# Turning three more expert steps' x by transposing DMAs in a fused linear-attention and mixture-of-experts kernel

## The chip, the cores and the metric

The kernel runs on one core of a Trainium2 chip. The metric is the device time of one execution in microseconds (us). The median of 3 runs before the change is 637.44 us (637.18 to 638.03).

## What is computed

The reference is a linear attention with random features, followed by a top-1 mixture of experts over all 4608 tokens. Everything is float32.

```python
def phi(x):                                    # q and k, scaled; omega: 128 x 64
    h = einsum('bhsd,md->bhsm', x, omega) - sum(x * x) / 2
    return exp(h - max(h)) / sqrt(m)
kv, z = einsum('bhsm,bhsd->bhmd', k_p, v), sum(k_p, axis=2)
attn = (q_p @ kv) / (q_p @ z + 1e-06)          # 8 x 8 x 576 x 64
x = attn.transpose(0, 2, 1, 3).reshape(4608, 512)

logits = normalised(x) @ normalised(expert_emb).T / tau    # 8 experts
expert_idx = argmax(logits, axis=1)
gate_w = softmax(logits)[arange(N), expert_idx]
for e in range(8):
    mask = expert_idx == e
    h = maximum(x[mask] @ w1[e], 0.0)                      # 512 -> 1024
    out[mask] = gate_w[mask, None] * (h @ w2[e])           # 1024 -> 512
```

## The kernel before

The first part computes the attention and scatters each token's row of x to a buffer in HBM (`xs`), sorted by expert. The second part, which the change touches, is a row of expert steps. A step takes 128 token rows of one expert. Steps 0 and 1 run inside the first part; the loop at L1177 runs steps t = 2 to 37 (`NPRE` = 2, `NSTAT` = 38).

Every float32 product is made of three: each operand is split into a high part and a low part (`xh`, `xl`; `hh`, `hl`; `w1h`, `w1l`, `w2h`, `w2l`), and `products` (L274) issues high by high, high by low-weight, and low by high-weight, for each of four slices of 128 rows. Half of a step's hidden layer is thus 12 matmuls of 512 columns, `pa[0]` and then `pa[1]` (`pb` in the trace), and the product with w2 is 24 (`po`). The first two matmuls of a half need only `xh`, the third needs `xl`.

TensorE contracts over partitions, so x must be turned (128 rows x 512 columns into four 128 x 128 blocks, transposed) and so must h. There are two ways to do it:

- On TensorE: `x_turned` (L1032) calls `turned` (L263): four transposes into a PSUM bank, ScalarE writes `xh` (L267), VectorE writes `xl` (L268).
- By DMA: `apart16` (L1078) copies the upper and lower 16 bits of every float32 into two planes `pl_1` and `pl_0`; `turned16` (L1086) issues one transposing DMA for each plane on SyncE's queue (L1090), into `t_k_0` and `t_k_1` of step k; in the next step `rejoin` (L1098) puts the two halves together in `wd`, and `summed` (L1113) makes `xh` (L1116), `hh` (L1118), `xl` (L1121) and `hl` (L1122).

Step t's own h goes by DMA in all steps but the first and the last. Where `far` holds, x of step t + 2 rides along in the same two planes, as 4 more blocks beside the 8 of h; elsewhere x of the next step is turned on TensorE between the two halves of a step. These are the lines:

```python
far = XPE <= t + 2 < NSTAT                                                 # L1179
planes = None if near else [... f"pl{t}_{k}", tag=f"pl{k}", bufs=1 ...]    # L1219
if t == NPRE or NPRE + 1 < t < XPE - 1:
    xt[t + 1] = x_turned(t + 1, xg[t + 1])                                 # L1223
if far:
    apart16(xg[t + 2][:, 0:DM], planes, F)                                 # L1232
if t == SHIFT:
    inverted(totals[0])
    ended()
elif t != SHIFT:
    down(u, both)                                                          # L1270
xg[t + 3] = x_of(t + 3, reg("row", t + 3))                                 # L1278
```

The order on every engine is the order in which the code is written. The product with w2 runs one step behind the one with w1 (`u = t - 1`) until step 4 and two steps behind from step 6 on. Step 5 (`SHIFT` = 5) has none: its 24 matmuls with w1 are followed directly by those of step 6. In its place step 5 scales the results of steps 2 and 3 on VectorE (`ended`, L291) ahead of `summed`. x of step t + 3 is loaded (`xgp` or `xg` from `xs`, L186) at the end of step t, behind that step's two transposing DMAs on the same queue.

Of the kernel before, what the change touches and what calls it, by code (L numbers as in the profile page):

```python
# [52 lines left out]
FILL1, FILL2, FILL3 = 2, 4, 8  # L53
NSTAT = 38
NSTEP = 64
XPE = 9
SHIFT = 5
BIGID = 1048576.0
EPS = 1e-6 * M
# [5 lines left out]
def attention_moe(ctx: ExitStack, tc: tile.TileContext, qT, kT, v1, omT, emb, tau, w1q, w2q, xs, out):  # L65
# [148 lines left out]
    def computed(wn, t, ms):  # L214
        for m in ms:
            seq[m] = len(seq)
        for o in range(NSTAT):
            apart(wn, spl.get((wn, o), ()), o, ms, t)
        if t >= NQ and (wn, t) not in mmi:
            for w in spl[wn, t - 1]:  # L220
                tc.add_manual_dep(ms[0].ins, w.ins.name, sync, reason="the weights")
        mmi.setdefault((wn, t), []).extend(ms)
# [51 lines left out]
    def products(dst, a, wn, par, cs, half, begin, end):  # L274
        ah, al = a
        _, wh, wl = W[wn]
        done = []
        for i, c in enumerate(cs):
            for k, (x, w) in enumerate(((ah, wh), (ah, wl), (al, wh))):
                if wn == "w1":  # L280
                    ws = w[:, ds(par, 1), c, half * 512 : (half + 1) * 512]
                else:
                    ws = w[:, ds(par, 1), c // 2, (c % 2) * 512 : (c % 2 + 1) * 512]
                done.append(nc.tensor.matmul(  # L284
                    dst, x[:, c * P : (c + 1) * P], ws.rearrange("p o f -> p (o f)"),
                    start=(begin and i == 0 and k == 0), stop=(end and i == len(cs) - 1 and k == 2),
                ))
        return done
# [743 lines left out]
    def x_turned(t, xg):  # L1032
        xh, xl = sums(t, "x", DM)
        turned(xg, 0, bank(f"pt{t}", "px", 2), xh, xl)
        return xh, xl
# [58 lines left out]
    with tc.manual_schedule(engines={ET.PE, ET.Activation, ET.DVE, ET.Pool, ET.SP}):  # L1094
# [82 lines left out]
        for t in range(NPRE, NSTAT):  # L1177
            u = t - 1 if t < SHIFT else t - 2
            far = XPE <= t + 2 < NSTAT  # L1179
            near = t in (NPRE, ends)  # L1180
# [41 lines left out]
            computed("w1", t, products(pa[0], xt[t], "w1", par, low, 0, True, True))  # L1222
            if t == NPRE or NPRE + 1 < t < XPE - 1:  # L1223
                xt[t + 1] = x_turned(t + 1, xg[t + 1])
# [139 lines left out]
```

## Time and profile before

| | |
|---|---|
| median of 3 runs | 637.44 us |
| profiled execution, its own time | 641.91 us |
| its span, first to last instruction | 640.3 us |
| TensorE (PE) busy | 627.2 us, 98% of the span |
| VectorE (DVE) busy | 491.8 us, 77% |
| ScalarE (ACT) busy | 431.8 us, 67% |
| GpSimd (POOL) busy | 420.6 us, 66% |
| mean granted TensorE clock | 0.998 of full |

The profiled execution is one execution, 4.5 us above the median of the others; its span is 1.6 us shorter than its own time. Times in views count from the start of the span. An engine's busy time does not count its waits; where a row ends with [a time <- a name], the engine was idle for that long ahead of it, and the name is what released it. Matmuls overlap in the pipeline, so the start of one to the start of the next is their cost, not the length shown.

### The profile page before, as it was taken

The page shows a single profiled execution, that of the slowest core. Times are in us where ns is not written, and L with a number is a line of the kernel's source. Part 1 is how long each engine was busy: PE and PEld are TensorE (multiplying, and loading weights), DVE is VectorE, ACT ScalarE, POOL GpSimd, SP SyncE. Part 2 cuts the span into 40 slices and gives each one's busy share as a digit, 9 for nine tenths or more (in the row PEclk, how much of TensorE's full clock was granted, in tenths as well). Part 3 has the DMA queues.
Part 4 walks back from the last instruction along what each step waited for, and adds up shares of the span by engine and source line. Part 5 has one row for each costly group of instructions (what it writes and reads, how often), then busy time and mean ns, then how long its engine had stood idle before and what let it go on. Part 6 is the DMA issues. An engine that isn't in the chain of part 4 may idle for free.

```text
span 640.3 us, 19056 instructions
## 1 busy us (share of the span) xinstructions
PE 627.2 (98%) x6289; PEld 535.4 (84%) x6290; DVE 491.8 (77%) x908; ACT 431.8 (67%) x1139; POOL 420.6 (66%) x603
## 2 busy tenths in 40 slices
PE   9999999999999899999999999999999999999996
PEld 8899999988888688888888888888888888888885
DVE  5688888898879755687778887787778786878754
ACT  6898898898988426755666675757565756666630
POOL 3012443355777644569789797979797979798852
PEclk9999999999999999999999999999999999999999
DMA  7655664767772277978877788686869686878631
GB/s 255 199 153 163 216 209 154 233 203 229 271 270 100 101 239 275 264 183 242 210 237 200 210 232 245 185 256 172 245 184 236 208 237 200 229 218 216 201 116 46
DMA packets 142239, 131.93 MB, mean 206 GB/s; under 512 B 106742, under 2 KB 106870, under 8 KB 142144
## 3 DMA queue, kind: packets, MB, share of 16 engines
q1 hardware_dynamic: 135520, 109.70, 59.7%
q0 software_dynamic: 6480, 20.91, 8.4%
q8 instruction: 57, 0.93, 0.6%
q14 instruction: 38, 0.31, 0.2%
q10 hardware_dynamic: 144, 0.07, 0.0%
HBM read 83.78 MB, written 21.97 MB: 165 GB/s over the span
## 4 chain that ended last, share of the span: by engine, by line
PE 70%; ACT 2%; DVE 1%; DMA 1%; issue 0%; POOL 0%; ACTq 0%
PE pb L284 31%; PE po L284 31%; PE fs_o L284 2%; PE pb L373 1%; PE nuu L481 1%; ACT ftq L387 1%; PE pb L266 1%; PE fs_a L284 1%; DMA rf<-w2q 1%; PE kva L405 1%; PE pb L461 0%; DVE nmq L377 0%; DVE xr L500 0%; PE nuu L538 0%; PE nuu L461 0%
## 5 line engine op out<-in xcount | busy, mean ns | idle before, releaser
L239 POOL TENSOR_TENSOR w2l<-raww,w2h 128x256 f32 x128 | 143.3, 1120 | 7.6
L239 POOL TENSOR_TENSOR w1l<-raww,w1h 128x256 f32 (+1 forms) x130 | 112.5, 865 | 14.5 <-DMA xgp<-xs 5.2
L284 PE MATMUL po<-w2h,hh 128*128 (+1 forms) x288 | 112.2, 390 | 0.0
L284 PE MATMUL po<-w2h,hl 128*128 (+1 forms) x288 | 112.1, 389 | 0.0
L284 PE MATMUL po<-w2l,hh 128*128 (+1 forms) x288 | 112.1, 389 | 0.0
L284 PE MATMUL pb<-w1h,xh 128*128 (+1 forms) x280 | 109.4, 391 | 0.0
L284 PE MATMUL pb<-w1h,xl 128*128 (+1 forms) x280 | 109.0, 389 | 0.0
L284 PE MATMUL pb<-w1l,xh 128*128 (+1 forms) x280 | 109.0, 389 | 0.0
L1084 DVE COPY pl<-pb 128x512 uint16<-128x512 uint16 x68 | 46.7, 689 | 60.2 <-ACT pl L1080 55.9
L1080 ACT ACTIVATE pl<-pb 128x512 uint16<-128x512 uint16 x68 | 39.4, 585 | 76.3 <-PE pb L284 66.5
L314 POOL DMA_INDIRECT y<-xgp,tail x36 | 45.0, 1250 | 55.2 <-DVE w1h L233 28.8
L387 ACT ACTIVATE ftq<-pb,nmq 128x128 f32<-128x128 f32 x288 | 79.6, 429 | 2.2 <-DVE nmq L377 1.3
L387 ACT ACTIVATE ftk<-pb,nmk 128x128 f32<-128x128 f32 x272 | 76.6, 479 | 6.0 <-DVE nmk L377 4.3
L1102 DVE COPY wd<-t 128x1024 uint16<-128x1024 uint16 x68 | 65.4, 963 | 1.6 <-DMA t<-pl 1.5
L1118 ACT ACTIVATE hh<-wd 128x1024 fp32r<-128x1024 f32 x34 | 36.1, 1063 | 42.7 <-DVE wd L1102 38.1
L284 PEld LDWEIGHTS po<-w2h,hh 128*128 128x128 f32 x288 | 54.1, 188 | 11.2
L284 PEld LDWEIGHTS po<-w2l,hh 128*128 128x128 f32 x288 | 54.1, 188 | 11.2
L284 PEld LDWEIGHTS po<-w2h,hl 128*128 128x128 f32 x288 | 54.0, 187 | 11.2
L284 PEld LDWEIGHTS pb<-w1h,xl 128*128 128x128 f32 x280 | 52.6, 188 | 11.0
L284 PEld LDWEIGHTS pb<-w1l,xh 128*128 128x128 f32 x280 | 52.6, 188 | 10.9
L284 PEld LDWEIGHTS pb<-w1h,xh 128*128 128x128 f32 x280 | 52.5, 187 | 10.7
L1122 DVE SCALAR_TENSOR_TENSOR hl<-wd,hh 128x1024 fp32r<-128x1024 f32 x34 | 54.2, 1594 | 4.0 <-ACT hh L1118 3.4
(341 smaller groups left out, 1250.4 us busy)
## 6 DMA issues: line engine op xcount, KB each, us to landing
raww<-w1q SPq DMA_DIRECT2D x38, 512.0 KB
raww<-w2q SPq DMA_DIRECT2D x38, 512.0 KB
qt<-qT SPq DMA_DIRECT2D x36, 256.0 KB
kt<-kT SPq DMA_DIRECT2D x35, 256.0 KB
xg<-xs SPq DMA_DIRECT2D x23, 260.5 KB
xgp<-xs SPq DMA_DIRECT2D x15, 260.5 KB
rf<-w1q SPq DMA_DIRECT2D x4, 512.0 KB
rf<-w2q SPq DMA_DIRECT2D x4, 512.0 KB
```

The lines of the kernel that those rows point to most:

```text
L239: ils.append(eng.tensor_tensor(at(l, d)[:, c], raw[:, c], at(h, d)[:, c].bitcast(F32), op=ALU.subtract))
L266: nc.tensor.transpose(bank[:, c * P : (c + 1) * P], src[:, o + c * P : o + (c + 1) * P], ident)
L284: done.append(nc.tensor.matmul(dst, x[:, c * P : (c + 1) * P], ws.rearrange("p o f -> p (o f)"), start=(begin and i == 0 and k == 0), stop ...
L314: w = nc.gpsimd.indirect_dma_start(out=out, out_offset=bass.IndirectOffsetOnAxis(ap=(xg[:, DM:] if tail is None else tail)[:, E : E + 1].b ...
L373: nc.tensor.matmul(st["pj" + w, i, a][:, c, :], st[w, i][r, c, :], om[r, :], start=True, stop=True)
L387: nc.scalar.activation(ft[:, h, :], pj[:, h, :], AF.Exp, bias=nm[:, h : h + 1])
L405: nc.tensor.matmul(acc[c : c + 64, h, :], ft[:, h, c : c + 64], vt[:, 2 * h + a, :], start=begin and h == 0, stop=u == 4 + 4 * b and h == 3,)
L1080: nc.scalar.activation(planes[1][:, o : o + 512], halved(src)[:, :, 1], AF.Copy)
L1084: nc.vector.tensor_copy(planes[0][:, o : o + 512], halved(src)[:, :, 0])
L1102: nc.vector.tensor_copy(to, src)
L1118: nc.scalar.activation(hh, wd[:, 0:F], AF.Relu)
L1122: nc.vector.scalar_tensor_tensor(hl, wd[:, 0:F], 0.0, hh.bitcast(F32), op0=ALU.max, op1=ALU.subtract)
```

## The change

The constant that says from which step on x is turned by DMA goes from 9 to 6.

```diff
@@ -53,7 +53,7 @@
 FILL1, FILL2, FILL3 = 2, 4, 8
 NSTAT = 38
 NSTEP = 64
-XPE = 9
+XPE = 6
 SHIFT = 5
 BIGID = 1048576.0
 EPS = 1e-6 * M
```

So x of steps 6, 7 and 8 (x6, x7, x8) are no longer turned on TensorE in steps 5, 6 and 7, but ride in the planes of steps 4, 5 and 6. The transposing DMAs of those steps carry 12 blocks where they carried 8. The three `turned` calls go: 12 transposes on TensorE, three L267 on ScalarE, three L268 on VectorE. For each of the three, ScalarE gets two plane copies of x (L1080, L1082), two rejoining copies (L1104) and `xh` (L1116), and VectorE gets `xl` (L1121).

VectorE's queue in step 5 before, from the weight copy that opens the step to the last instruction for step 4's h (`pb` the PSUM banks, `po` the results of steps 2 and 3):

```order
L233 COPY w1h<-raww_5_5426 128x1024
L268 TENSOR_TENSOR xl_5655<-pb_74,xh_5654 128x512
L1084 COPY pl_0_5640<-pb_72 128x512
L1102 COPY wd_5676<-t_4_0_5581 128x1024
L1084 COPY pl_0_5640<-pb_73 128x512
L1102 COPY wd_5676<-t_4_1_5583 128x1024
L307 TENSOR_SCALAR totalb_5628<-totalb_5628 128x3
L308 RECIPROCAL totalb_5628<-totalb_5628 128x3
L291 TENSOR_SCALAR xgp_135<-po_5378,totalb_5628 128x512
L291 TENSOR_SCALAR xgp_136<-po_5587,totalb_5628 128x512
L1122 SCALAR_TENSOR_TENSOR hl_5696<-wd_5676,hh_5695 128x1024
```

The same queue at the same place after the change:

```order
L233 COPY w1h<-raww_5_5426 128x1024
L1084 COPY pl_0_5642<-pb_72 128x512
L1102 COPY wd_5672<-t_4_0_5583 128x1024
L1084 COPY pl_0_5642<-pb_73 128x512
L1102 COPY wd_5672<-t_4_1_5585 128x1024
L307 TENSOR_SCALAR totalb_5630<-totalb_5630 128x3
L308 RECIPROCAL totalb_5630<-totalb_5630 128x3
L291 TENSOR_SCALAR xgp_135<-po_5378,totalb_5630 128x512
L291 TENSOR_SCALAR xgp_136<-po_5589,totalb_5630 128x512
L1121 TENSOR_TENSOR xl_5694<-wd_5672,xh_5693 128x512
L1122 SCALAR_TENSOR_TENSOR hl_5697<-wd_5672,hh_5696 128x1024
```

The low part of x6 was the second of these rows and is now the tenth, behind the plane copy of the step's second half (the second L1084).

ScalarE's queue in step 5 after the change, from the last gate of the step to `hh` (`xg_5193` holds x7, `t_4` the turned planes of step 4; before, one L267 and the two L1080 from `pb` stood ahead of L1118):

```order
L304 ACTIVATE ex_5635,totalb_5630<-tail_5423,nrmb_5624 128x8
L1080 ACTIVATE pl_1_5643<-pb_72 128x512
L1080 ACTIVATE pl_1_5643<-xg_5193 128x512
L1082 ACTIVATE pl_0_5642<-xg_5193 128x512
L1104 ACTIVATE wd_5672<-t_4_0_5583 128x512
L1104 ACTIVATE wd_5672<-t_4_1_5585 128x512
L1080 ACTIVATE pl_1_5643<-pb_73 128x512
L1116 ACTIVATE xh_5693<-wd_5672 128x512
L1118 ACTIVATE hh_5696<-wd_5672 128x1024
```

Five rows are new here, and the copies of x7 now stand ahead of the second half's plane copy.

## Rows read from the trace of the kernel before

**Rows 1.** The page's first part: busy us, share, instructions of each engine.
```profile
PE 627.2 (98%) x6289; PEld 535.4 (84%) x6290; DVE 491.8 (77%) x908; ACT 431.8 (67%) x1139; POOL 420.6 (66%) x603
```

**Rows 2.** Waits of TensorE, longest first: total us, times, longest.
```profile
PE nuu L481 <- DVE base L551: 1.6, 1, 1.6
```

**Rows 3.** Chain that ended last, steps 4 to 8: start us, us, what.
```profile
262.87 5.44 PE po L284 x24
268.31 2.73 PE pb L284 x12
271.04 0.44 PE pb L266 x4
271.48 5.51 PE pb L284 x24
...
285.63 2.72 PE pb L284 x12
...
297.00 5.44 PE pb L284 x24
```

**Rows 4.** SyncE's queue in time order: x6's load, step 4's transposing DMAs.
```profile
258.96 0.33 SPq L186 DMA_DIRECT2D xgp<-xs  x1
...
265.10 2.61 SPq L1090 DMA_TRANSPOSE t<-pl  x2
```

**Rows 5.** ScalarE in time order, steps 4 and 5: start us, us, operation.
```profile
262.98 1.07 ACT L1080 ACTIVATE pl<-pb 128x512 uint16<-128x512 uint16 x2
...
266.07 0.60 ACT L295 ACTIVATE nuu<-xgp 128x512 f32<-128x512 f32 x1
...
268.99 0.19 ACT L304 ACTIVATION_READ_ACCUMULATOR ex<-tail,nrmb 128x1 f32 x1
```

**Rows 6.** L186 (loads of x), 240 to 300 us: issue to landing.
```profile
DMA to landing us min/median/max: 3.1/5.1/7.0
```

**Rows 7.** ScalarE in step 8, where x already goes by DMA.
```profile
300.30 0.62 ACT L1080 ACTIVATE pl<-xg 128x512 uint16<-128x512 uint16 x1
...
301.35 1.41 ACT L1104 ACTIVATE wd<-t 128x512 uint16<-128x512 uint16 x2
...
303.08 0.63 ACT L1116 ACTIVATE xh<-wd 128x512 fp32r<-128x512 f32 x1
```

**Rows 8.** VectorE in step 8, from the second half's plane copy.
```profile
303.21 0.69 DVE L1084 COPY pl<-pb 128x512 uint16<-128x512 uint16 x1 [1.41 <-ACT pl L1080]
...
304.46 1.21 DVE L1121 TENSOR_TENSOR xl<-wd,xh 128x512 fp32r<-128x512 f32 x1
```

**Rows 9.** VectorE in step 5: what follows its last rejoining copy.
```profile
276.16 0.16 DVE L307 TENSOR_SCALAR totalb<-totalb 128x3 f32<-128x3 f32 x1
...
276.56 1.41 DVE L291 TENSOR_SCALAR xgp<-po,totalb 128x512 f32<-128x512 f32 x2
```

**Rows 10.** SyncE's queue in a later step: transposing DMAs, next load.
```profile
467.13 3.00 SPq L1090 DMA_TRANSPOSE t<-pl  x2
470.70 0.34 SPq L186 DMA_DIRECT2D xg<-xs  x1
```

**Rows 11.** ScalarE behind the DMAs of rows 10, in time order.
```profile
473.84 0.60 ACT L1080 ACTIVATE pl<-pb 128x512 uint16<-128x512 uint16 x1 [2.60 <-DMA t<-pl]
474.81 0.63 ACT L1080 ACTIVATE pl<-xg 128x512 uint16<-128x512 uint16 x1 [0.37 <-DMA xg<-xs]
```

**Rows 12.** Stretches: us, busy of PE, PEld, DVE, ACT, POOL; clock, DMA share, GB/s.
```profile
635.00:637.80 2.80, 0.18 (x1) 0.00 (x0) 0.00 (x0) 0.69 (x1) 1.14 (x2) 1.00 0.02 7
637.90:640.00 2.10, 0.00 (x0) 0.00 (x0) 0.00 (x0) 0.00 (x0) 0.00 (x0) 0.50 0.30 106
```

**Rows 13.** TensorE's first matmuls, L91 and L373: ns min/median/max, first to last start.
```profile
L91 PE MATMUL pb<-one x24: 289/314/314, 1.3 to 3.7; 128*128 128x128 bf16 x24
...
L373 PE MATMUL pb<-om,kt x18: 417/418/578, 4.1 to 6.2; 64*128 64x128 f32 x18
...
L373 PE MATMUL pb<-om,kt x34: 272/272/462, 6.2 to 11.9; 64*128 64x128 f32 x34
```

## Prediction

> **What bounds the kernel now.** I read the busy times first: TensorE is busy for 98% of the span, no other engine for more than 77% [rows 1]. Then its waits: the longest single one is 1.6 us, in the attention part [rows 2], so in the expert steps it hardly waits at all. Then the chain that ended last, from step 4 to step 8 [rows 3]: it is TensorE without a gap, one row's end being the next one's start. Step 4's product with w2 runs from 262.87, step 5's first half from 268.31, x6's four transposes at 271.04, then 24 matmuls that are step 5's second half and, with nothing between, step 6's first. So each us taken from TensorE here is a us gained, and each us it waits is lost, since no later row shows idle time that could give it back.
>
> **What is removed.** Step 7, with transposes, goes from 285.63 to 297.00: 11.37 us. A step without them is twice the 5.44 us of 24 matmuls [rows 3], 10.88 us. That is 0.49 us a step (0.44 of transposes and a little of a slower restart), 1.47 us for three. ScalarE's L267 and VectorE's L268 that went with them were off the path.
>
> **What is added, and where it is late.** In a step from 8 on, x of two steps ahead has a step and a half to be turned. The place to look at is step 5, which has no product with w2: x6's new path must fit between step 4's planes and step 6's first half, and the latter is due right behind step 5's second half. Without transposes step 5's 24 matmuls go from 268.31 to 273.75 [rows 3], so step 6's third matmul, the first that needs the low part of x6, is due at 273.75 + 0.45 (two matmuls of 0.227) = 274.2. I follow x6 to that point.
>
> 1. *x6 must be in.* Its load is issued at 258.96 [rows 4]. Loads of x in this stretch take 3.1 to 7.0 us [rows 6], so it lands no earlier than 262.1; ScalarE reads it at 266.07 without a wait [rows 5], which is the upper bound. The new plane copies stand behind the first of two L1080 that start at 262.98, so they want x6 at 263.5. I take a landing at 265.0, near the upper end, because two weight loads stand just ahead of it in the queue.
> 2. *Step 4's planes.* Two copies of x take 1.05 us (300.30 to 301.35 in step 8 [rows 7]): 265.0 to 266.05; the second half's own copy about 0.55 [rows 5]: 266.6. VectorE's copy of the same half waits for ScalarE's each time [rows 8], and takes 0.69: the planes are full at 267.3, and SyncE issues the transposes at 267.4 instead of 265.10 [rows 4]. ScalarE's remaining work of the step, which ended at 269.18 [rows 5], moves by about 2.3 too, to 271.5, where the first half of step 5 is ready (268.31 + 2.73 + 0.4).
> 3. *x7's load* is queued behind the transposes on SyncE. In a later step it is issued 3.57 us after them [rows 10], so at 271.0 here. There ScalarE was held by it until 474.81, 4.1 us after its issue [rows 11]; the least in this stretch is 3.1 [rows 6]. I take 3.1, since only a short queue is left at this point: 274.1. The planes themselves are free once the transposes have read them, at most 6.7 us after their issue (467.13 to 473.84 [rows 10, 11]) and thus no later than x7.
> 4. *ScalarE in step 5.* x7's copies 274.1 to 275.1, the two rejoining copies for x6 1.3 (301.35 to the next start, of 1.41 [rows 7]): 276.4, the second half's plane copy 0.55: 276.9.
> 5. *VectorE in step 5.* Its plane copy and rejoining copy take 1.25 up to the start of the next (303.21 to 304.46 [rows 8]); then come the totals and the two scalings of finished results, 276.16 to 277.97 = 1.81 [rows 9]; then x6's low part, 1.21 [rows 8]. Sum 4.27: 281.2.
>
> So step 6's third matmul starts at 281.2 instead of 274.2: TensorE waits 7.0 us, in two pieces around two early matmuls (xh6 is there at about 277.5, from the 0.63 us of rows 7). Of this, at least 4.8 us need no DMA to be late: step 5's second half ends at 273.75 + 0.4, and 0.55 + 4.27 us of copies behind it in the two queues end at 279.0. The net is 7.0 - 1.47 = +5.5 us. With x6 in by 263.5 and x7 3.1 us after its issue the same sum ends at 279.7 (+4.0); with x6 at 266.07 and x7 4.1 us after its issue it ends at 283.2 (+7.5).
>
> **What is late next.** h of step 4 follows x6 by one VectorE instruction and is used only after step 6's 24 matmuls, 5.4 us later: covered. x7's low part, by the same chain (x8's load issued at about 281.2, 4.1 us to land, then 1.05 + 1.3 + 0.55 + 1.25 + 1.21), is there at 290.7; step 6 has its product with w2 again, so step 7's third matmul is due at 281.2 + 2.3 + 2.7 + 5.4 + 0.45 = 292.1. That cover is 1.4 us; were it gone, each us would be paid. x8 in step 7 is as the steps from 8 on. GpSimd's splitting of the weights waits for the two scalings and moves with them by about 2 us, TensorE by more. The growth of the transposing DMAs from 8 to 12 blocks is in the times of step 3 of the sum, which are those of 12 blocks [rows 10, 11].
>
> **The clock.** At the end of the run TensorE's last matmul reaches 0.18 us into the stretch from 635.00, and from 637.90 on the granted clock reads 0.50, the lower level of 1.2 GHz; over the stretches before it, it is 1.00, and the wait of 1.6 us [rows 2] did not lower it [rows 12]. The wait that I forecast is of 7 us with two matmuls in it, far nearer to the end of the run than to the 1.6 us. What a fall costs: at the start TensorE works from 1.3 us, its L373 take 418 ns until 6.2 and 272 after [rows 13]. Those 4.9 us at half speed bound the loss at 2.5 us; below it is nothing. I take 1.8, nearer to the start's case.
>
> The Trainium skill, TensorE: Matmul & The Clock Gate, section What's actually happening, says that the throttled state is the default and activity lifts it. The end of this trace agrees (0.50 after the last matmul). By that rule the sum is 5.5 + 1.8 = 7.3 us; by the shorter wait's row alone it would stay at 5.5.
>
> **The sum.** On the profiled execution's own 641.91 us: 641.91 + 7.3 = 649.2. On the median, which is 4.5 us lower and holds the same instructions: 637.44 + 7.3 = 644.7 us. Within 0.2% (1.3 us) of 637.44 a measurement of this kernel could hardly tell a change from none.
>
> **The rivals.**
> - *The wait comes, the clock holds.* Two matmuls in the middle of the wait speak for it, the end of the run against it. 642.9 us.
> - *All is hidden.* x6's low part is in time, and TensorE gains its transposes: 637.44 - 1.47 = 636.0. For it: from step 8 on the same path causes no wait, and VectorE and ScalarE have idle time. Against it: it decides at a wait of 1.47 us, that is at xl6 written by 275.7, and VectorE's queue puts it behind a copy that cannot start before step 5's second half has ended at 274.1; it would take 1.6 us for what the rows cost at 4.8.
> - *Only the part that needs no late DMA.* x6 and x7 land early in the changed traffic: wait 4.8 us, net +3.3, so 640.8 with the clock held and 642.6 with a fall.
> - *It spreads.* x7 is late for step 7 too, because x8's load lands 7.0 us after its issue rather than 4.1: 2.9 us later against 1.4 of cover, 1.5 us more, 646.2.
>
> **How the numbers follow.** The wait with a fall of the clock: 0.55, its own range 642.5 to 646.5. The wait, clock held: 0.2. Only the unavoidable part: 0.12. Spread: 0.06. Hidden: 0.04, and 0.03 for something that ends within 0.2%. Range 640.8 to 646.6: it leaves out the hidden and unchanged cases and half of the spread one. Slower 0.93, same 0.03, faster 0.04.
>
> **What would show it.** In the changed trace, TensorE idle ahead of step 6 for 5 to 9 us in all, ended by VectorE's L1121; ScalarE's L1080 on x6 and x7 each with a wait for the load; transposes of step 4 issued near 267.4; steps 6 to 8 at 10.88 us each where the clock is 1.00; a stretch at 0.50 behind the wait. If the gap is under 2 us, the reading of step 5's queues is wrong. If the clock stays at 1.00, only its term is.

## The result and the profile after

The changed kernel takes 645.09 us, median of 5 runs (643.46 to 646.48), and the one before, run beside it, 637.3 (637.14 to 638.03): a ratio of 1.0114, 95% interval 1.0101 to 1.0128. By the medians the change costs 7.8 us, by the ratio 7.3. The forecast was 644.7 in 640.8 to 646.6.

The profiled execution took 643.46 us, with a span of 641.9, only 1.6 more than that of before. In the page's busy line TensorE has 3.3 us less than in [rows 1] and ScalarE 8.4 more.

```profile
PE 623.9 (97%) x6277; PEld 532.9 (83%) x6278; DVE 493.2 (77%) x908; ACT 440.2 (69%) x1151; POOL 420.1 (65%) x603
```

The spans can't be set against each other as they stand. These are the first matmuls of step 4's product with w2 and of step 5, before:

```profile
262.71 0.39 PE L284 MATMUL po<-w2h,hh 128*128 128x512 f32 x1
...
268.15 0.39 PE L284 MATMUL pb<-w1h,xh 128*128 x1
```

And after:

```profile
258.21 0.39 PE L284 MATMUL po<-w2h,hh 128*128 128x512 f32 x1
...
263.65 0.39 PE L284 MATMUL pb<-w1h,xh 128*128 x1
```

All that comes ahead of step 4's product, which the change does not touch, went 4.5 us faster in this execution. (The chain of [rows 3] puts each start 0.16 us later than the matmul's own row.) From that product to the end of the span it is 641.9 - 258.21 = 383.7 us after and 640.3 - 262.71 = 377.6 before. The change costs 6.1 us in this execution.

TensorE's waits, longest first (total us, times, longest): both of the first two are new, the wait of 1.6 us in [rows 2] is of 0.4 us in this execution.

```profile
PE pb L284 <- issue: 3.0, 1, 3.0
PE pb L284 <- DVE xl L1121: 1.9, 1, 1.9
```

TensorE in order of time around them. The first row is step 5's last matmul, the second and third are step 6's first two, the fourth is the third matmul, which needs the low part of x6; the row behind it shows the pitch then, and the last is the first of step 6's product with w2.

```profile
268.87 0.39 PE L284 MATMUL pb<-w1h,xl 128*128 x1
272.21 0.77 PE L284 MATMUL pb<-w1h,xh 128*128 x1 [2.96 <-issue]
272.78 0.63 PE L284 MATMUL pb<-w1l,xh 128*128 x1
275.32 0.79 PE L284 MATMUL pb<-w1h,xl 128*128 x1 [1.92 <-DVE xl L1121]
...
276.34 0.63 PE L284 MATMUL pb<-w1l,xh 128*128 x1
276.77 0.63 PE L284 MATMUL pb<-w1h,xl 128*128 x1
...
282.07 0.39 PE L284 MATMUL po<-w2h,hh 128*128 x1
```

Step 5 begins at 263.65. The third matmul of step 6 was due 5.44 (24 matmuls) + 0.45 = 5.89 us later, at 269.54. It starts at 275.32: a wait of 5.8 us. From there to the product with w2 are 22 matmuls, 4.99 us at 0.227, and they take 6.75: another 1.76 us, since for a part of them the pitch is 0.43. Less the 1.47 us of transposes the sum is 5.8 + 1.76 - 1.47 = 6.1 us, all that the span from step 4's product on shows.

SyncE, ScalarE and VectorE in the same stretch, in order of time. SyncE issues step 4's transposing DMAs, then x7's load:

```profile
262.74 2.88 SPq L1090 DMA_TRANSPOSE t<-pl  x2
265.86 0.38 SPq L186 DMA_DIRECT2D xg<-xs  x1
```

ScalarE takes x6 in the first row as its load lands, then waits for the transposing DMAs to leave the planes, then for x7's load; x6's rejoining, the second half's plane copy and `xh` follow.

```profile
260.35 0.63 ACT L1080 ACTIVATE pl<-xgp 128x512 uint16<-128x512 uint16 x1 [0.99 <-DMA xgp<-xs]
...
267.71 0.60 ACT L1080 ACTIVATE pl<-pb 128x512 uint16<-128x512 uint16 x1 [0.87 <-DMA t<-pl]
268.73 0.63 ACT L1080 ACTIVATE pl<-xg 128x512 uint16<-128x512 uint16 x1 [0.42 <-DMA xg<-xs]
269.27 0.61 ACT L1082 ACTIVATE pl<-xg 128x512 uint16<-128x512 uint16 x1
269.79 1.38 ACT L1104 ACTIVATE wd<-t 128x512 uint16<-128x512 uint16 x2
271.03 0.57 ACT L1080 ACTIVATE pl<-pb 128x512 uint16<-128x512 uint16 x1
271.50 0.62 ACT L1116 ACTIVATE xh<-wd 128x512 fp32r<-128x512 f32 x1
```

VectorE waits for that plane copy, and x6's low part stands behind the two scalings:

```profile
271.63 0.69 DVE L1084 COPY pl<-pb 128x512 uint16<-128x512 uint16 x1 [1.94 <-ACT pl L1080]
272.24 0.74 DVE L1102 COPY wd<-t 128x1024 uint16<-128x1024 uint16 x1
...
273.26 1.41 DVE L291 TENSOR_SCALAR xgp<-po,totalb 128x512 f32<-128x512 f32 x2
274.59 0.68 DVE L1121 TENSOR_TENSOR xl<-wd,xh 128x512 fp32r<-128x512 f32 x1
```

Read backwards, this is the chain that the prediction followed: `xl` behind the scalings, behind the copies, behind ScalarE, behind x7's load. TensorE's first wait, for which the view names only "issue", is ScalarE's `xh`: it ends at 272.12, and the matmul starts at 272.21.

The granted clock, in stretches (us, busy of PE, PEld, DVE, ACT, POOL; clock, DMA share, GB/s):

```profile
262.00:269.20 7.20, 7.20 (x33) 5.66 (x31) 5.19 (x9) 5.72 (x16) 5.04 (x6) 1.00 0.81 207
269.20:272.00 2.80, 0.05 (x1) 0.00 (x0) 0.86 (x2) 2.80 (x6) 1.04 (x1) 1.00 0.10 38
272.00:275.30 3.30, 1.19 (x2) 0.50 (x2) 3.23 (x8) 2.39 (x6) 0.99 (x1) 0.50 0.59 133
275.30:278.80 3.50, 3.48 (x8) 2.80 (x9) 2.48 (x3) 1.09 (x2) 3.13 (x3) 0.50 1.05 265
278.80:282.20 3.40, 3.40 (x16) 2.77 (x16) 1.37 (x2) 2.67 (x5) 3.17 (x5) 1.00 0.99 358
```

At 272.0 it falls to 0.50, the lower level of 1.2 GHz, and it is back at 2.4 GHz from 278.8. In the last row but one 8 matmuls fill 3.48 us; in the last 16 fill 3.40.

From step 6's product with w2 on, the steps have no wait any more, and step 7 takes 10.88 us (5.44 + 5.44), as a step without transposes has to (start us, us, what):

```profile
282.23 5.44 PE po L284 x24
287.67 5.44 PE pb L284 x24
293.11 5.44 PE po L284 x24
```

### The profile page after: what moved, and what is told of

It is laid out like the page before. It is cut to its first block, busy times and chain, and to the rows that moved or that the text cites. A ratio compares the mean times of both kernels' runs of the same rounds, so it can differ in the third digit from the quotient of the medians.

```text
span 641.9 us, 19044 instructions
## 1 busy us (share of the span) xinstructions
PE 623.9 (97%) x6277; PEld 532.9 (83%) x6278; DVE 493.2 (77%) x908; ACT 440.2 (69%) x1151; POOL 420.1 (65%) x603
## 4 chain that ended last, share of the span: by engine, by line
PE 63%; ACT 4%; DVE 2%; DMA 2%; issue 2%; POOL 1%; SPq 0%; DVEq 0%; ACTq 0%; POOLq 0%
PE po L284 29%; PE pb L284 28%; PE fs_o L284 2%; PE pb L373 1%; ACT ftq L387 1%; PE nuu L481 1%; DMA xgp<-xs 1%; DMA raww<-w2q 1%; PE fs_a L284 1%; PE kva L405 1%; DMA xg<-xs 0%; DVE nmq L377 0%; POOL w2l L231 0%; POOL y L314 0%; ACT pl L1080 0%
## 5 line engine op out<-in xcount | busy, mean ns | idle before, releaser
L239 POOL TENSOR_TENSOR w2l<-raww,w2h 128x256 f32 x128 | 143.1, 1118 | 7.6
L239 POOL TENSOR_TENSOR w1l<-raww,w1h 128x256 f32 (+1 forms) x130 | 111.8, 860 | 14.5 <-DMA xgp<-xs 4.8
L1084 DVE COPY pl<-pb 128x512 uint16<-128x512 uint16 x68 | 46.9, 691 | 68.7 <-ACT pl L1080 68.7
L1080 ACT ACTIVATE pl<-pb 128x512 uint16<-128x512 uint16 x68 | 39.6, 584 | 76.6 <-PE pb L284 75.6
L1102 DVE COPY wd<-t 128x1024 uint16<-128x1024 uint16 x68 | 68.4, 1009 | 1.2 <-DMA t<-pl 1.2
L1118 ACT ACTIVATE hh<-wd 128x1024 fp32r<-128x1024 f32 x34 | 36.1, 1062 | 40.8 <-DVE wd L1102 36.6
## 6 DMA issues: line engine op xcount, KB each, us to landing
xg<-xs SPq DMA_DIRECT2D x23, 260.5 KB, 2.9
xgp<-xs SPq DMA_DIRECT2D x15, 260.5 KB, 3.4
```

What stands on the lines that cost most here:

```text
L239: ils.append(eng.tensor_tensor(at(l, d)[:, c], raw[:, c], at(h, d)[:, c].bitcast(F32), op=ALU.subtract))
L1080: nc.scalar.activation(planes[1][:, o : o + 512], halved(src)[:, :, 1], AF.Copy)
L1084: nc.vector.tensor_copy(planes[0][:, o : o + 512], halved(src)[:, :, 0])
L1102: nc.vector.tensor_copy(to, src)
L1118: nc.scalar.activation(hh, wd[:, 0:F], AF.Relu)
```

## The experiments

The first theory: x6 is late because step 5 has no product with w2; only x6 is, so with x7 and x8 by DMA alone the kernel gains two steps' transposes. The rivals: every x costs a third of the loss; x7 is late as well, hidden behind x6's wait; or the clock and not the wait is most of the loss. All edits below are to the changed kernel, unless another is named; a line of dots stands for lines left out. The ratios are to the kernel before, run beside each, and are not the quotients of the two medians (e7's is 0.1% below its quotient): its medians were 637.54 us for e1 to e4, 637.96 for e5 to e8, 638.12 for e9 to e11 and 638.23 for e12.

| run | us, median (range) | ratio, 95% interval |
|---|---|---|
| e1, DMA from x7 on | 642.3 (639.15 to 644.02) | 1.0076, 1.0061 to 1.0091 |
| e2, from x8 on | 638.29 (637.08 to 639.77) | 1.0007, 0.9998 to 1.0017 |
| e3, x6 but not x7, x8 | 645.41 (644.12 to 646.51) | 1.0113, 1.0098 to 1.0129 |
| e4, filling matmuls, shared tile | 650.22 (649.37 to 651.31) | 1.0196, 1.0181 to 1.0212 |
| e5, filling matmuls, free bank | 642.43 (641.96 to 642.84) | 1.0072, 1.0059 to 1.0085 |
| e6, scalings behind `summed` | 643.45 (641.89 to 643.67) | 1.0076, 1.0064 to 1.0089 |
| e7, x6 rejoined first | 643.49 (640.0 to 646.06) | 1.0077, 1.0051 to 1.0103 |
| e8, x6 and x7 first | 639.97 (638.45 to 642.45) | 1.0029, 1.0017 to 1.004 |
| e9, all x first, from x6 | 639.25 (637.78 to 643.15) | 1.0018, 1.0004 to 1.0032 |
| e10, all x first, from x7 | 638.83 (636.82 to 640.8) | 1.0011, 0.9998 to 1.0024 |
| e11, all x first, from x9 | 637.9 (637.0 to 639.29) | 0.9993, 0.9984 to 1.0003 |
| e12, as e9, w1 split earlier | 638.34 (637.05 to 644.48) | 1.0004, 0.998 to 1.0028 |

**Which x is late: e1, e2, e3.**

```diff
-XPE = 6
+XPE = 7
```

> The constant is 7: x6 is turned on TensorE again, x7 and x8 go by DMA. Theory (the wait is x6's alone, because step 5 has no product with w2 to cover its path): no wait, two times 0.49 us of transposes gained, 636.3 us beside 637.3 before. Rival (every x that goes by DMA in these early steps costs a third of the 7.8 us lost, through busier queues): 642.5.

The theory failed: x7 and x8 by DMA cost 4.8 us (642.3 - 637.5), and it is x7, since x8 alone costs nothing that can be told (e2). In e1's trace TensorE waits before step 7, twice. The first row is step 6's last matmul:

```profile
279.95 0.39 PE L284 MATMUL po<-w2h,hl 128*128 x1
282.12 0.47 PE L284 MATMUL pb<-w1h,xh 128*128 x1 [1.77 <-POOL w2l L239]
...
283.50 0.50 PE L284 MATMUL pb<-w1h,xl 128*128 x1 [0.68 <-DVE xl L1121]
```

ScalarE shows the same order as before step 6, one step later, with 1.73 us of waiting for x8's load:

```profile
278.62 0.63 ACT L1080 ACTIVATE pl<-xg 128x512 uint16<-128x512 uint16 x1 [1.73 <-DMA xg<-xs]
...
281.40 0.62 ACT L1116 ACTIVATE xh<-wd 128x512 fp32r<-128x512 f32 x1
```

The first wait is put down to GpSimd, but its row (279.05, 3.16 us) runs to 282.21, past the matmul's start; `xh` of x7 ends at 282.02, 0.10 us ahead of it, and is what it waited for. Step 7's third matmul was due three matmuls behind the first row, at 280.63, and comes at 283.50: 2.9 us late. (The idle times in the rows are shorter, since they count from the end of a matmul's own length.) Less 0.98 of transposes that is 1.9 us. In the profiled execution the clock held, and from step 4's product with w2 on it is 2.1 us longer than before (637.6 - 257.92 = 379.7); that execution is the run of 639.15. The other runs show a mean clock of 0.996 to 0.997. A fall of the clock would explain a part of the median's further 2.7 us: e7's trace, below, has a mean clock of 0.997 and loses 1.7 us by one. No trace of e1's other runs was taken, so the rest is open.

```diff
-XPE = 6
+XPE = 8
```

> The constant is 8: only x8 goes by DMA. Theory: one time 0.49 us gained, 636.8 us, which is only just to be told from 637.3. Rival (a third of the loss for each x): 639.9.

With x8 alone there is no wait in the steps, and the rest of the span is 635.7 - 258.57 = 377.1 us, 0.5 less than before, one step's transposes. The medians don't show it: 1.0007, and the interval reaches from a small gain to a loss of 0.17%.

```diff
-XPE = 6
+XPE = 9
...
-            far = XPE <= t + 2 < NSTAT
+            far = XPE <= t + 2 < NSTAT or t + 2 == 6
...
-            if t == NPRE or NPRE + 1 < t < XPE - 1:
+            if t == NPRE or NPRE + 1 < t < XPE - 1 and t + 1 != 6:
```

> Only x6 goes by DMA, x7 and x8 are turned on TensorE. Theory: nearly the whole loss stays. ScalarE is no longer held by x7's load in step 5, so the wait is some 1.2 us shorter than the 5.8 of the changed kernel, the clock falls as there for some 1.8, and 0.49 is gained: 4.6 + 1.8 - 0.5, 643.2 us. Rival (a third for each x): 639.9.

x6 alone costs as much as all three (645.41 against 645.09), in place of 643.2 expected. The wait is what it was expected to be without x7's load in ScalarE's queue: the third matmul is 4.5 us late, in the two pieces below, where the first again is `xh` (272.69 for 0.62 us), not GpSimd.

```profile
273.41 0.47 PE L284 MATMUL pb<-w1h,xh 128*128 x1 [1.68 <-POOL w1l L239]
...
276.53 0.80 PE L284 MATMUL pb<-w1h,xl 128*128 x1 [2.41 <-DVE xl L1121]
```

So x7's load and its two plane copies in ScalarE's queue are worth 5.8 - 4.5 = 1.3 us of x6's wait. The rest came from the clock: it fell to 0.50 in the second wait and stayed there through step 6's first half; less the 0.49 us of transposes, what the 4.5 us leave of this execution's +6.6 is some 2.5 us for it. (From step 4's product with w2 on it is 644.9 - 260.70 = 384.2 us long, 6.6 more than before.) Together: x7 (with x8) costs 4.8, x6 alone 7.9 (645.41 - 637.5), all three 7.8 (645.09 - 637.3). That is not a third for each x, though e1 came near that rival's 642.5. The waits don't add, since x6's wait gives x7 the time that it lacks (e7 shows it).

**Is the clock's part separate: e4, e5.** 96 matmuls of 128 columns fill TensorE's wait. They leave the results alone. This is e5's edit:

```diff
+            if t == SHIFT + 1:
+                for _ in range(96):
+                    nc.tensor.matmul(pa[1][:, 0:P], one16, one16, start=True, stop=True)
```

In e4 they stood at the end of step 5 and wrote into `nu[1]`.

> The changed kernel with 96 matmuls of 128 columns into an unused PSUM bank between step 5 and step 6, about 5 us of work in a wait of 5.8; they leave the results alone. Theory (the wait and the lower clock behind it are two costs): the clock stays at 1.00, the wait stays, and the time is lower by about 1.8 us than the changed kernel's 645.1, so 643.3. Rival (the clock costs nothing that the wait does not cost already): 645.1. A third possibility is that the matmuls themselves end after the low part of x6 is there; then the time is higher by what they overrun.

It missed its aim: `nu[1]` is the tile into which ScalarE's squares (L295) write, so the added matmuls waited 5.84 us for these and then ran for 8.29 us on the path. It tells nothing of the clock. e5 writes into a bank that is free there.

> The changed kernel with the 96 added matmuls of 128 columns written into the bank of step 6's second half, which nothing reads at that time, ahead of step 6's first matmul. At the 56 ns from start to start that they took at the clock of 1.00 they are 5.4 us in a wait of 5.8. Theory: no clock below 1.00 behind step 5, the low part of x6 comes when it came, the time is lower by the 1.8 us of the clock than 645.1: 643.3. Rival (the clock costs nothing that the wait does not cost): 645.1.

In e5's trace the mean clock is 1.00, so it did not fall in the steps:

```profile
core 0: 640.4 us, clock 1.000
```

TensorE around the filler:

```profile
269.11 5.53 PE L1224 MATMUL pb<-one 128*128 128x128 bf16 x96
...
275.44 0.50 PE L284 MATMUL pb<-w1h,xl 128*128 x1 [0.28 <-DVE xl L1121]
```

The third matmul starts as late as without the filler: 11.8 us behind step 5's first (263.66), against 11.7. The median falls by 645.09 - 642.43 = 2.7 us (the ratio by 0.0042, the same 2.7). From step 4's product with w2 on, the profiled execution is 640.4 - 258.22 = 382.2 us long, 1.5 less than the changed kernel's. So the clock is a term by itself: 1.5 to 1.8 us by the rows of the profiled executions, 2.7 by the medians.

**Is it the order in the queues: e6, e7, e8.** e6 puts the scalings behind `xl`:

```diff
-            if t == SHIFT:
-                inverted(totals[0])
-                ended()
 ...
+            if t == SHIFT:
+                inverted(totals[0])
+                ended()
```

> The changed kernel with the two scalings of step 5 and their totals behind step 4's h on VectorE instead of ahead of x6's low part. Theory (VectorE's queue is part of the wait): the low part comes 1.7 us sooner, 645.1 - 1.7 = 643.4. Rival (the DMAs alone decide when it comes): 645.1.

The median falls by 1.6 us, as expected, and the third matmul comes 10.1 us behind step 5's first (264.06), in place of 11.7: the two scalings stood in x6's way.

```profile
274.18 0.79 PE L284 MATMUL pb<-w1h,xl 128*128 x1 [0.68 <-DVE xl L1121]
```

But a fall of the clock has no fixed price. From the third matmul to the product with w2, at 282.18, e6's 22 matmuls take 8.0 us in place of 4.99: the lower clock costs 3.0 us in this execution, where it cost 1.76 in the changed kernel's. So from step 4's product on e6's is 642.0 - 258.62 = 383.4 us long, only 0.3 less. It is the slowest of e6's six runs.

e7 moves x6's rejoining, `xh` and `xl` ahead of the first plane copy of step 5, and so ahead of x7's load too:

```diff
+                if t in (5,):
+                    wd6 = words(t - 1)
+                    for k in range(2):
+                        rejoin(t - 1, wd6, F, F + DM, k)
+                    xt[t + 1] = xh, xl = sums(t + 1, "x", DM)
+                    nc.scalar.activation(xh, wd6[:, F:], AF.Copy)
+                    nc.vector.tensor_tensor(xl, wd6[:, F:], xh.bitcast(F32), op=ALU.subtract)
                 apart16(pa[0], planes, 0)
...
```

> The changed kernel with x6's rejoining copies, its high and its low part ahead of all plane copies in step 5. Step 4's transposing DMAs landed 2 us before step 6's first half was due, so the DMAs do not forbid it. Theory (the order of the two queues, not the DMAs, makes x6 late): x6's wait falls from 5.8 to about 0.7 us. x7's wait in front of step 7, which the one in front of step 6 hid, comes out then, some 3 us as in the kernel with the constant 7, some of its runs with a fall of the clock: 637.5 - 1.5 + 0.7 + 3.3 = 640.0, with a fall 641.5. Rival (the DMAs make x6 late): 645.1.

x6 is in time, and x7's wait comes out, as e1 foretold, with the clock at 0.50 for a stretch behind it. TensorE's rows are before step 6 (one wait) and before step 7 (two):

```profile
273.00 0.50 PE L284 MATMUL pb<-w1h,xh 128*128 x1 [0.87 <-POOL w1l L239]
...
285.43 0.47 PE L284 MATMUL pb<-w1h,xh 128*128 x1 [1.25 <-POOL w2l L239]
...
286.99 0.79 PE L284 MATMUL pb<-w1h,xl 128*128 x1 [0.86 <-DVE xl L1121]
```

The wait before step 6 is not x6's any more. Its low part (L1235, from 271.67, 0.69 us) is written at 272.36, where it was due at 266.53 + 5.89 = 272.42; GpSimd's low part of the next w1 ends at 272.94:

```profile
269.32 3.62 POOL L239 TENSOR_TENSOR w1l<-raww,w1h 128x256 f32 x4 [1.30 <-DVE w1h L233]
```

By the matmuls' starts GpSimd costs 1.2 us there, x7 2.5 before step 7 (the first of these two waits is again ended by `xh`, which is written at 285.33), and the lower clock 1.7. Less 1.47 of transposes that is 3.9, which is what e7's profiled execution shows from step 4's product with w2 on (642.6 - 261.09 = 381.5 us).

e8 does the same in steps 5 and 6 (`t in (5, 6)`).

> As the kernel with x6 first, and the same order in step 6 for x7. Theory: x7's wait goes too, since its transposing DMAs land some 2 us ahead of step 7; 637.5 - 1.5 + 0.7 = 636.7, the transposes' gain nearly whole. Rival (x7 waits for its DMAs): 640 to 641.5.

Now x7 is in time, and x8 is late before step 8; the wait for GpSimd before step 6 is left too (1.36 us):

```profile
295.49 0.50 PE L284 MATMUL pb<-w1h,xl 128*128 x1 [1.32 <-DVE xl L1121]
```

**What is late once every x is early: e9 to e12.** e9 uses that order in every step in which x of the next comes by DMA; e10 the same with `XPE = 7`; e11 with `XPE = 9`, where x6 to x8 are turned on TensorE and only the order is new. Against e7 the test for the step differs:

```diff
-                if t in (5,):
+                ahead = late and not early and XPE <= t + 1 < NSTAT
+                if ahead:
```

> The changed kernel with every x that goes by DMA rejoined and split ahead of the plane copies, in all steps and not in steps 5 and 6 alone. With x6 and x7 in time, x8 waited 1.3 us in front of step 8, behind the plane copies and the load of x9 in step 7. Theory (the queue order makes x late wherever TensorE does not wait before it): only x6's wait of about 1.2 us is left, no fall of the clock in most runs: 637.9 - 1.5 + 1.2 = 637.6. Rival (the two engines and the DMAs have too much to do in these steps, whatever the order; the wait moves on to a later step): about 640 as with x6 and x7 first.

> The same order with the constant 7: x6 on TensorE, x7 and x8 by DMA. Theory: no wait at all, two times 0.49 gained: 636.9 beside 637.9 before. Rival (the wait moves on): 638.5 to 640.

> The kernel before, constant 9, with the same order in its steps from 8 on: what the order by itself does. Theory: nothing, since no x was late there: the time of before within 0.2%. If the order costs or gains something by itself, it shows here and is to be taken off the other two.

The order alone does nothing (e11: 0.9993). e9 is left with 1.1 us more than before, 1.2 by the profiled execution (637.5 - 258.71 = 378.8 us). The wait before step 6, and GpSimd's row that ends it, at 271.00:

```profile
271.06 0.50 PE L284 MATMUL pb<-w1h,xh 128*128 x1 [1.30 <-POOL w1l L239]
```

```profile
267.35 3.65 POOL L239 TENSOR_TENSOR w1l<-raww,w1h 128x256 f32 x4 [1.30 <-DVE w1h L233]
```

Here the name is right: x6 is ready, and the low part of the next w1 ends 0.06 us before the matmul starts. GpSimd waited for VectorE's `w1h`, which stands behind the gate's work on ScalarE and VectorE. From step 5 to step 10 TensorE loses 2.6 us by the matmuls' starts, 1.6 of them before step 6 and the rest in smaller pieces (one is named, 0.20 us for `w1l` before step 9), which outweighs the 1.47 of transposes by 1.1. In e10 the same wait (1.51 us) stands before step 8. e12 splits w1 ahead of the gate's work, in the order of e9:

```diff
+            if SHIFT <= t < ends:
+                split("w1", t)
...
-            if t not in (NPRE + 1, ends):
+            if t < SHIFT and t != NPRE + 1:
                 split("w1", t)
```

> The kernel that rejoins every x ahead, constant 6, with each step's split of the weights for w1 (from step 5 on) moved ahead of the gates' norms and of the scaling and store of finished results on VectorE and GpSimd. What TensorE still waited for there was GpSimd's low part of w1: 1.3 us in front of step 6, 0.2 in front of step 9. Theory (after x is in time, the weights' low parts are what the work of steps 4 to 7 on VectorE makes late): these waits go, and the gain of the three transposes shows at last: 638.1 - 1.3 = 636.8. Rival (the path of DMAs, copies and splits from step to step is itself longer than a step once TensorE does not wait, and the wait moves to another of its parts): 638.5 to 639.3 as before this edit.

That wait is gone, but another stands in its place. The chain in e12's trace, from step 5 to step 6:

```profile
268.07 5.44 PE pb L284 x24
273.51 0.52 issue
274.03 5.96 PE pb L284 x24
```

It is x6 again. ScalarE writes `xh` at 273.93 and VectorE `xl` at 274.65, where step 6's third matmul was due at 267.91 + 5.89 = 273.80. With the split first, the gate's small operations on VectorE end later, ScalarE's gates wait 1.01 us for them (until 271.00), and x6's rejoining stands behind the gates. From step 5's first matmul to step 6's product with w2 it is 279.82 - 267.91 = 11.9 us for 48 matmuls of 10.88: 1.0 us is lost there, which leaves some 0.4 of the 1.47 us of transposes. From step 4's product with w2 to the end it is 639.9 - 262.47 = 377.4 us, 0.2 less than before, and the ratio is 1.0004 with an interval from -0.2 to +0.28%. The rival was the nearer of the two: the wait moved to another part of the path. No version beats the kernel before by what can be measured.

## Why the prediction was right, and where it was not

- *Which x and which queues*: right for the changed kernel. The chain from x6's landing to `xl` holds row by row, best in its first half. By the matmuls' rows step 5 began 4.50 us earlier in this execution (263.65 against 268.15). With that taken off, x6 was forecast to land at 260.5 and ScalarE starts on it at 260.35; the transposes were forecast to be issued at 262.9 and were at 262.74. That the missing product with w2 makes step 5 the one place to look at was wrong: x7, in step 6, is late as well once x6 is not (e1, e7).
- *The size of the wait*: 5.8 us in place of 7.0. Three terms of step 3 to 5 of the sum were too long. x7's load was issued 3.12 us after the transposes, not 3.57; it held ScalarE until 2.87 us after its issue, not 3.1; and `xl` itself took 0.68 us, not the 1.21 of [rows 8]. These are 0.45 + 0.23 + 0.53 = 1.2 us.
- *The part that needs no late DMA* (4.8 us): e3, without x7's load, measured 4.5; with `xl` at its 0.68 us the forecast would have been 4.3.
- *The clock*: it fell, as the likeliest case had it. The rule that the prediction draws on, from the Trainium skill, TensorE: Matmul & The Clock Gate, section What's actually happening, agrees with the trace: 0.50 behind an idle TensorE, 1.00 again behind matmuls in a row. The term of 1.8 us was 1.76 in the profiled execution, but that it was so near is partly luck: e6's trace has 3.0, e3's 2.5, and e5 against the changed kernel makes it 2.7 by the medians. Its bound was read from the lengths of the first matmuls alone; the profile shows no granted clock below 1.00 in that stretch. That the median lies within 0.4 us of the forecast is luck too: a wait 1.2 us too long in the sum was offset by a median that lies 1.7 us above the profile's +6.1. Why the other executions are slower than the profiled one, at the same mean clock of 0.994, is open; the attention part differs by some us between executions of either kernel.
- *What is late next*: half right. In the changed kernel x7 is covered: `xl` of x7 ends at 285.45 and is due at 282.07 + 5.44 + 0.45 = 287.96, 2.5 us in place of 1.4. But this cover is x6's own wait, which puts step 7 off. e1 and e7 take that wait away and x7 is late by 2.9 and 2.5 us. The prediction counted "step 6 has its product with w2 again" as the cover; that was not enough. x8 "as the steps from 8 on" held in the changed kernel and in e1, not in e8. GpSimd's splits behind the scalings moved by 1.8 us, as forecast, and TensorE by more. But the split of w1 ahead of them moved by 1.8 us too, which the prediction does not count: it ends 6.6 us behind step 5's start (270.24) where it was 4.8, in part because GpSimd's split before it starts 0.9 us later: it needs ScalarE's `w2h`, which stands behind the copies of x6 in step 4. x6's wait covers it in the changed kernel; where x6 comes before it (e7, e8, e9) TensorE waits 1.2 to 1.7 us for it.
- *The gain of transposes* (1.47 us): it fits the sum of the profiled execution. As a faster kernel it was not shown.

## What to carry to other kernels

Where work moves from the bounding engine to a path through in-order queues, count the time from its source to its use at the step with the least work between, and count everything that stands ahead of it in each queue, loads for later steps too. Then take the first wait away on paper and look again: a wait covers the ones behind it, here x7's, x8's and GpSimd's split of w1 in turn. A wait of TensorE can cost more than its length, so forecast the clock as a term of its own, with a range: here one fall cost between 1.7 and 3.0 us.

## What the runs showed of the hardware that was not expected

- The granted clock fell in the first piece of TensorE's wait, ahead of the two matmuls at 272.21 and 272.78 on which the rival with the clock held had rested: it reads 1.00 until 272.0, and the last matmul had started at 268.87. It stayed at 0.50 until 278.8, 3.5 us after the matmuls had come back in a row at 275.32, and there they started 0.43 us apart instead of 0.227. In e9 a wait of 1.30 us left it at 1.00, and in e1 two of 1.77 and 0.68 us; in e7, behind two of 1.25 and 0.86 us, it fell. Why it fell there and not in e1 is open.
- VectorE's `xl` has two times in the trace of the changed kernel (ns, shortest, median, longest):

```profile
L1121 DVE TENSOR_TENSOR xl<-wd,xh x32: 681/1220/1231, 274.6 to 610.6; 128x512 fp32r<-128x512 f32 x32
```

The short one is x6's, with none of GpSimd's splits (L239) running; each of the other 31 has a split beside it and takes 1.21 to 1.23 us. The low parts of x7 in e1 and e7, also with no split beside them, take 0.68. The Trainium skill, SBUF — State Buffer, section Who interferes with whom, says that a VectorE instruction with two inputs in SBUF contends with a GpSimd instruction that reads SBUF; `xl` has two such inputs, and the trace agrees. A split beside it does not always lengthen `xl`: in e7 x6's, at 271.67, takes 0.69 us while splits run from 269.32 to 272.94, and in e9 the times range from 0.69 to 4.02 us. What decides it was not tested. The prediction's 1.21 was read from a step in which GpSimd was splitting, and in step 5 GpSimd itself waits for the scalings.
- A small operation can be hit harder. In the changed kernel one of the gate's on VectorE, with two inputs of 128x3, takes 2.41 us beside a GpSimd split of 2.40 us, and 0.16 us two steps later without one:

```profile
263.02 2.41 DVE L1155 TENSOR_TENSOR nrmb<-nrmb,roughb 128x3 f32<-128x3 f32 x1
...
287.02 0.16 DVE L1155 TENSOR_TENSOR nrmb<-nrmb,roughb 128x3 f32<-128x3 f32 x1
```

```profile
263.01 2.40 POOL L231 TENSOR_TENSOR w2l<-raww,w2h 128x1024 fp32r<-128x1024 f32 x1 [0.62 <-ACT w2h L229]
```
